# Operand moves two per tile and later loads in the attention stage of a three-stage kernel

## The chip, the cores and the metric

One core of a Trainium2 chip runs the kernel. The metric is the device time of one execution in microseconds (us), the median of several runs. The profile is one further execution, recorded by the hardware profiler, with the time of every instruction from the start of the span.

## The reference, cut to what matters

```python
# attention: B=2, H=8, S=768, D=64
q_bits = (einsum('bhsd,dk->bhsk', q, proj) > 0); k_bits likewise     # 6 bits
mask = q_bucket[..., :, None] == k_bucket[..., None, :]
scores = where(mask, matmul(q, k^T) / sqrt(D), -1e9)
x = softmax(scores) @ v            # -> [1536, 512]
# first expert layer: all 8 experts, weighted by a Sinkhorn-balanced P
x = sum_e P[:, e] * (relu(x @ w1[e]) @ w2[e])
# second expert layer: each token goes to one expert, 192 tokens each
out[mask_e] = relu(x[mask_e] @ w1b[e]) @ w2b[e]
```

The change touches the attention alone. Heads with other buckets are not cut away: the bucket test is added to the scores as 64 further rows of the product.

## The kernel before

The attention works on *pairs* of heads. There are 8 pairs (n = 0 to 7), each with 12 *tiles* (r = 0 to 11): 2 heads by 6 blocks of 128 queries. Tile t of the whole run is 12n + r; the main loop (L408 on) has 96 of them and some more to drain the pipeline. In each tile the table PLANS says in which order the steps are written, and with which lag; the engines follow that order by hand, each in its own queue, with waits only where data or a buffer demand it. The steps that matter here:

- `qk` (L283): TensorE (PE) makes the scores S from two operand pairs, S<-ka,qa and S<-kb,qb. The operands of a pair of heads are four tiles qa, ka, qb, kb of 128 rows, kept twice (`ST`), so that the next pair's are built while this pair's are read.
- `soft`, `expo`, `inv`, `norm`: VectorE (DVE) takes the maximum, ScalarE (ACT) the exponential, DVE the reciprocal w (L302), GpSimd (POOL) multiplies e by w (L307).
- `tr` (L315): PE transposes e; ACT and DVE split it into ah and al; `av` (L337): PE makes O.
- `xa` with a lag of 8 tiles: ACT copies O to SBUF and SyncE (SP) issues the *exchange* DMAs that put the two heads' halves together. For the second head of a pair the copy goes to one of three tiles in turn, x1, idle and pz (L357), and two DMAs of 64 KB follow, xm<- (L358) and xc<- (L359). These fall in r = 2, 4 and 6 of the next pair. For the first head it is one DMA xc<-xm (L353), in r = 8, 10 and 0.
- `xp` with a lag of 10: POOL adds xm and xc (L369) and splits the sum (L370, L371), in r = 4, 6 and 8, ahead of work that stands later in POOL's queue, `norm` above all.
- `pp`, `pa`, `pd`: the next pair is prepared in r = 0 to 9. r = 0 and 1 transpose and split the next q into qhi and qlo, r = 2 and 3 the next k into khi and klo; r = 4 and 5 take the bits, r = 6 to 9 make the rows of the bucket test, `hot`. `stack` puts 6 *moves* of 64 x 768 floats (192 KB, SBUF to SBUF) into the list MOVES for q in r = 1, and 6 for k in r = 3. After a tile's steps `move` issues (L165) all moves that were in the list before the tile began. The hot rows go by DMAs of their own (L241): qb<-hot twice in r = 7, kb<-hot twice in r = 9.
- `pv`: the loads of q, k and v of the next pair but one, `load(n + 2, ...)`, two DMAs of 192 KB each (L82), in r = 6, 7 and 10. Pairs 6 and 7 have no such loads. In r = 6, `pv` stands ahead of `xa` in the plan.

All these DMAs are issued by SP from one queue in program order. SP waits for nothing but what an instruction needs, so it is not bound to the tiles; a DMA whose data is late keeps all behind it back.

Of the kernel before, what the change touches and what calls it, by code (L numbers as in the profile page):

```python
# [38 lines left out]
def rd(x):  # L39
    return x.bitcast(F32)  # L40
# [3 lines left out]
def kernel(ctx, tc, q, k, v, proj, wg1, w1, w2, wg2, w1b, w2b, out):  # L44
# [29 lines left out]
    def load(n, what="qkv"):  # L74
        b, hp = divmod(n, HP)
        for nm, src in (("q", q), ("k", k), ("v", v)):
            if nm in what:
                t = ap.tile([128, R, 2, D], F32, name="r" + nm, bufs=2)
                rows = (slice(0, R // 2), slice(R // 2, R)) if n == 0 and nm != "v" else (slice(0, R),)
                for rs in rows:  # L80
                    for s in range(2):
                        nc.sync.dma_start(t[:, rs, s, :], src[b, 2 * hp + s].rearrange("(p r) d -> p r d", r=R)[:, rs])  # L82
                RAW["r" + nm, n] = t
# [78 lines left out]
    def move(n=None):  # L162

        for dst, src in MOVES[:n]:
            nc.sync.dma_start(rd(dst), rd(src))  # L165
        del MOVES[:n]
# [86 lines left out]
    def prep_v(n, i):  # L253
        x = RAW["rv", n]
        if i == 0:
            VS[n] = ap.tile([128, R, 2, 2, D], F32R, name="vv", bufs=2)
        vv = VS[n]
        s = i // 2
        if i % 2 == 0:
            nc.gpsimd.tensor_tensor(vv[:, :, s, 0, :], x[:, :, s, :],  # L260
                                    zero[:, :, None].to_broadcast([128, R, D]), op=OP.add)
        else:
            nc.gpsimd.tensor_tensor(vv[:, :, s, 1, :], x[:, :, s, :], rd(vv[:, :, s, 0, :]), op=OP.subtract)
# [114 lines left out]
    def ahead_v(t):  # L378
        n, r = divmod(t, TU)
        for i in range(4):  # L380
            if t == PREP_V[i]:
                prep_v(0, i)
        if r in (8, 10) and n + 1 < NP:
            prep_v(n + 1, r // 2 - 4)
        if r in (0, 2) and 0 < n < NP:
            prep_v(n, r // 2 + 2)
        for what, at in (("q", 6), ("k", 7), ("v", 10)):
            if r == at and n + 2 < NP:
                load(n + 2, what)

    STEPS = dict(qk=qk, soft=soft, expo=expo, inv=inv, norm=norm, tr=tr, th=trh, tl=trl, av=av, xa=xa, xp=xp, pp=lambda t: ahead(t, 0), pa=lambda t: ahead(t, 1), pd=lambda t: ahead(t, 2),
                 pv=ahead_v)
    patterns()
    for i in (0, 1, 2, 3, 4, 5, 6, 8, 7, 9):
# [15 lines left out]
    for t in range(NT + max(x[1] for x in PLANS[0])):  # L410
        if t == TU:
            nc.vector.tensor_copy(wgs[:, :, :E], wgr)
            nc.vector.tensor_tensor(wgs[:, :, E:], wgr, rd(wgs[:, :, :E]), op=OP.subtract)
        due = len(MOVES)
        for nm, lag, *part in PLANS[t % 2]:
            if 0 <= t - lag < NT:
                STEPS[nm](t - lag, *part)
        if due:
            move(due)
    order.close()  # L420
    actx.close()

# [802 lines left out]
```

## Time and profile before

| what | value |
|---|---|
| median of 3 runs | 1595.63 us (1595.05 to 1595.82) |
| profiled execution: its own time | 1594.99 us |
| profiled execution: span from first to last instruction | 1591.6 us |
| PE busy | 1553.0 us (98%) |
| DVE, ACT, POOL busy | 809.0, 453.3, 272.7 us |
| attention stage in the span | about 0 to 280 us |

An engine's share is an average over all stages. A stall is read from the engine's timeline: a row there has the start and length of the instruction and, in brackets, how long the engine stood idle before it and which instruction or DMA ended that wait. "SPq" rows are DMA issues: their length is the time to issue, not the time to land.

### The profile page before, as it was taken

Reading aid. Unit: us, or ns where it says so; the run is one execution under the profiler, and the core shown is the slowest. Engines: PE = TensorE matmul, PEld = TensorE weight load, DVE = VectorE, ACT = ScalarE, POOL = GpSimd, SP = SyncE. Lnnn points to the kernel's source line nnn. Section 1 sums busy time; section 2 is a strip of 40 time slices with the busy share of each in tenths; the row PEclk is TensorE's granted clock in tenths of the full one; section 3 lists DMA queues with packets and bytes.
Section 4 is the critical chain, followed back from the end, with each engine's and each line's share of the span. In section 5 each row is a group of like instructions: output and inputs, shape, how many; then the busy total and the mean of one; then the engine's idle time right before and its main releaser. Section 6 shows DMA issues by size and latency. Waiting matters only on the chain.

```text
span 1591.6 us, 21436 instructions
## 1 busy us (share of the span) xinstructions
PE 1553.0 (98%) x8482; PEld 1318.1 (83%) x8482; DVE 809.0 (51%) x1833; ACT 453.3 (28%) x857; POOL 272.7 (17%) x316
## 2 busy tenths in 40 slices
PE   8889999999999999999999999999999999999998
PEld 7889887788888888888888888888887777888998
DVE  7878887721523324333342332134677377667533
ACT  7778886311210211221121021022121210011343
POOL 5778888020000000000000000000000000111221
PEclk9999999999999999999999999999999999999999
DMA  9657761220200110120020021011000115555531
GB/s 194 139 128 166 160 137 35 99 93 0 81 26 14 54 53 1 53 67 1 27 87 7 14 71 36 0 54 53 1 14 14 40 41 210 191 183 187 192 136 30
DMA packets 88871, 122.84 MB, mean 77 GB/s; under 512 B 44227, under 2 KB 51907, under 8 KB 88771
## 3 DMA queue, kind: packets, MB, share of 16 engines
q1 hardware_dynamic: 81280, 108.89, 23.8%
q0 software_dynamic: 2176, 6.29, 1.3%
q10 hardware_dynamic: 5314, 6.30, 1.1%
q8 instruction: 66, 1.08, 0.3%
q14 instruction: 35, 0.28, 0.1%
HBM read 83.91 MB, written 9.44 MB: 59 GB/s over the span
## 4 chain that ended last, share of the span: by engine, by line
PE 88%; DVE 3%; DMA 2%; ACT 2%; POOL 2%; issue 1%; SPq 1%; POOLq 0%; ACTq 0%; DVEq 0%
PE hp L575 32%; PE yp L594 29%; PE hp L952 5%; PE yp L896 4%; PE yp L1005 3%; PE tp L315 2%; PE O L337 2%; PE S L283 2%; PE yp L1008 1%; PE sp L1089 1%; POOL e L307 1%; PE tp L205 1%; ACT e L295 1%; PE tp L176 1%; PE yp L1010 1%
## 5 line engine op out<-in xcount | busy, mean ns | idle before, releaser
L575 PE MATMUL hp<-X,big 128*128 128x512 f32 x2304 | 530.5, 390 | 0.6 <-DVE big L445 0.6
L575 PEld LDWEIGHTS hp<-X,big 128*128 128x128 f32 x2304 | 432.9, 188 | 91.2 <-DVE big L445 1.0
L594 PE MATMUL yp<-big 128*128 128x512 f32 x2016 | 461.2, 389 | 0.0
L594 PEld LDWEIGHTS yp<-big 128*128 128x128 f32 x2016 | 378.2, 188 | 78.5
L576 ACT ACTIVATE big<-hp 128x512 fp32r<-128x512 f32 x176 | 105.2, 598 | 753.7 <-PE hp L575 753.7
L577 DVE SCALAR_TENSOR_TENSOR big<-hp,big 128x512 fp32r<-128x512 f32 x176 | 121.4, 690 | 250.3 <-ACT big L576 250.3
L599 DVE SCALAR_TENSOR_TENSOR acc<-yp,P,acc 128x512 f32<-128x512 f32 x72 | 54.1, 751 | 258.4 <-PE yp L594 258.4
L877 POOL DMA_INDIRECT raw<-x2h,who x4 | 4.2, 1038 | 949.4 <-DVE wg2b L1074 939.0
L307 POOL TENSOR_TENSOR e<-e,w 128x768 f32<-128x768 f32 x96 | 139.0, 1468 | 31.2 <-DVE w L302 24.6
L327 DVE TENSOR_TENSOR al<-tp,ah 128x512 fp32r<-128x512 f32 x144 | 98.4, 684 | 31.3 <-ACT ah L323 27.9
L315 PE MATMUL tp<-ident,e 128*128 128x128 f32 x576 | 87.5, 280 | 15.4 <-POOL e L307 15.3
L323 ACT ACTIVATE ah<-tp 128x512 fp32r<-128x512 f32 x144 | 86.4, 601 | 42.9 <-PE tp L315 40.4
L952 PE MATMUL hp<-raw,big 128*128 128x192 f32 x488 | 93.7, 338 | 1.2 <-ACT raw L930 1.2
L290 DVE TENSOR_REDUCE w<-S 128x1 f32<-128x768 f32 x96 | 91.3, 951 | 6.9 <-PE S L283 5.8
L295 ACT ACTIVATE e<-S,w 128x768 f32<-128x768 f32 x96 | 87.0, 907 | 2.1 <-DVE w L290 1.8
L315 PEld LDWEIGHTS tp<-ident,e 128*128 128x128 f32 x576 | 69.3, 145 | 17.9 <-POOL e L307 17.0
L952 PEld LDWEIGHTS hp<-raw,big 128*128 128x128 f32 x488 | 79.7, 193 | 2.7 <-ACT raw L930 1.6
L445 DVE TENSOR_TENSOR big<-raw,big 128x1024 fp32r<-128x1024 f32 x63 | 76.7, 1221 | 9.5 <-ACT big L444 9.5
L337 PE MATMUL O<-ah,vv 128*128 128x256 f32 x288 | 74.9, 289 | 1.3 <-ACT xm L352 0.9
L337 PE MATMUL O<-al,vv 128*128 128x256 f32 x288 | 74.7, 288 | 0.0
L444 ACT ACTIVATE big<-raw 128x1024 fp32r<-128x1024 f32 x63 | 64.8, 1053 | 31.4 <-DMA raw<-in_moe_w_dram 30.0
L550 DVE SCALAR_TENSOR_TENSOR junk<-acc,wg2b 128x512 bf16<-128x512 f32 x96 | 66.0, 688 | 1.9
(261 smaller groups left out, 1587.3 us busy)
## 6 DMA issues: line engine op xcount, KB each, us to landing
raw<-in_moe_w_dram SPq DMA_DIRECT2D x67, 512.0 KB, 3.5
big<-in_moe_w_dram SPq DMA_DIRECT2D x32, 1024.0 KB, 7.5
qa<-qhi SPq DMA_DIRECT2D x30, 192.0 KB, 3.8
ka<-klo SPq DMA_DIRECT2D x16, 192.0 KB, 3.4
rv<-in_v_dram SPq DMA_DIRECT2D x16, 192.0 KB, 4.4
x2h<-acc ACTq DMA_DIRECT2D x24, 128.0 KB, 1.9
x<-acc ACTq DMA_DIRECT2D x12, 256.0 KB, 3.2
qb<-qlo SPq DMA_DIRECT2D x15, 192.0 KB, 3.6
```

The costliest lines, as they stand in the source:

```text
L290: nc.vector.tensor_reduce(EN[t][:, 0, i:i + 1], Sp[i], op=OP.max, axis=AX.X, negate=True)
L295: nc.scalar.activation(e, Sp[i], AF.Exp, bias=w[:, 0, i:i + 1], scale=1.0, accum_out=w[:, 1, i:i + 1])
L307: nc.gpsimd.tensor_tensor(e, e, w[:, 3, i:i + 1].to_broadcast([128, S]), op=OP.mult)
L315: nc.tensor.transpose(p[:, y * 128:y * 128 + 128], EN[t + i][:, kt * 128:kt * 128 + 128], ident)
L323: nc.scalar.activation(ah, TP[t, x], AF.Copy)
L327: nc.vector.tensor_tensor(al, TP[t, x], rd(ah), op=OP.subtract)
L337: nc.tensor.matmul(o, VS[n][:, kt, s].rearrange("p a d -> p (a d)"), a[:, :, kt], start=(kt == 0 and a is ah), stop=(kt == R - 1 and a is al))
L575: nc.tensor.matmul(t, a, b, start=(i == 0), stop=(i == len(prods) - 1))
L576: nc.scalar.activation(hh[:, f], t, AF.Relu)
L577: nc.vector.scalar_tensor_tensor(hl[:, f], t, 0.0, rd(hh[:, f]), op0=OP.max, op1=OP.subtract)
L594: nc.tensor.matmul(t, a, b, start=(i == 0), stop=(i == len(prods) - 1))
L952: nc.tensor.matmul(opened[f], w[:, d, f * 128:f * 128 + 128], xt[:, d], start=(d == 0), stop=(d == HP - 1))
```

## The change

Two edits. The loads of the pair n + 2 move from r = 6, 7 and 10 to r = 8, 10 and 11 (the 9th, 11th and 12th tile of a pair). And after each tile at most two of the waiting moves are issued instead of all.

```diff
-        for what, at in (("q", 6), ("k", 7), ("v", 10)):
+        for what, at in (("q", 8), ("k", 10), ("v", 11)):
             if r == at and n + 2 < NP:
                 load(n + 2, what)
@@
-        if due:
-            move(due)
+        move(min(due, 2))
```

PE, DVE, ACT and POOL keep their order. SP's changes in pairs 0 to 6. In SP's queue in pair 1, from the idle exchange to the pz exchange (ka, kb, qa, qb are operand tiles of the next pair, rq the load of q), before:

```order
L358 DMA xm<-idle 64x256
L359 DMA xc<-idle 64x256
L165 DMA ka_119<-khi 64x768
L165 DMA ka_119<-klo 64x768
L165 DMA kb_121<-khi 64x768
L165 DMA ka_119<-khi 64x768
L165 DMA ka_119<-klo 64x768
L165 DMA kb_121<-khi 64x768
L82 DMA rq<-in_q_dram 128x6x64 x2
L358 DMA xm<-pz 64x256
L359 DMA xc<-pz 64x256
```

The same stretch in the change:

```order
L358 DMA xm<-idle 64x256
L359 DMA xc<-idle 64x256
L165 DMA qa_118<-qhi 64x768
L165 DMA qb_120<-qlo 64x768
L165 DMA ka_119<-khi 64x768
L165 DMA ka_119<-klo 64x768
L358 DMA xm<-pz 64x256
L359 DMA xc<-pz 64x256
```

Between the two exchanges stand four moves, where six moves and the two q loads stood; ahead of the idle exchange stand four moves, where there were six.

In SP's queue in pair 1, behind the pz exchange up to the hot rows of kb (rk is the load of k), before:

```order
L82 DMA rk<-in_k_dram 128x6x64 x2
L241 DMA qb_120<-hot_831 64x768 x2
L353 DMA xc<-xm 64x256
L241 DMA kb_121<-hot_906 64x768 x2
L82 DMA rv<-in_v_dram 128x6x64 x2
```

And in the change:

```order
L165 DMA kb_121<-khi 64x768
L165 DMA ka_119<-khi 64x768
L241 DMA qb_120<-hot_824 64x768 x2
L165 DMA ka_119<-klo 64x768
L165 DMA kb_121<-khi 64x768
L82 DMA rq<-in_q_dram 128x6x64 x2
L353 DMA xc<-xm 64x256
L241 DMA kb_121<-hot_903 64x768 x2
L82 DMA rk<-in_k_dram 128x6x64 x2
```

Four k moves and the q loads now stand between the pz exchange and kb<-hot; the k loads went behind it, and the v loads behind those.

## Rows read from the trace of the kernel before

**Rows 1.** The page, part 1: busy time, share, instructions of each engine.
```profile
PE 1553.0 (98%) x8482; PEld 1318.1 (83%) x8482; DVE 809.0 (51%) x1833; ACT 453.3 (28%) x857; POOL 272.7 (17%) x316
```

**Rows 2.** Waits of PE, 10 to 280 us: total us, times, longest.
```profile
PE tp L315 <- POOL e L307: 15.3, 7, 4.1
...
PE S L283 <- DMA kb<-hot: 2.3, 1, 2.3
```

**Rows 3.** Timeline of PE: start, us, instruction, [idle before, releaser].
```profile
42.31 0.58 PE L283 MATMUL S<-kb,qb 128*128 128x512 f32 x2 [2.33 <-DMA kb<-hot]
...
71.23 0.66 PE L315 MATMUL tp<-ident,e 128*128 128x128 f32 x4 [2.81 <-POOL e L307]
106.03 1.02 PE L315 MATMUL tp<-ident,e 128*128 128x128 f32 x4 [4.05 <-POOL e L307]
...
138.47 0.66 PE L315 MATMUL tp<-ident,e 128*128 128x128 f32 x4 [1.70 <-POOL e L307]
...
170.59 0.74 PE L315 MATMUL tp<-ident,e 128*128 128x128 f32 x4 [2.70 <-POOL e L307]
203.90 0.66 PE L315 MATMUL tp<-ident,e 128*128 128x128 f32 x4 [2.57 <-POOL e L307]
...
237.59 0.51 PE L283 MATMUL S<-kb,qb 128*128 128x512 f32 x2
```

**Rows 4.** Waits of POOL, 10 to 280 us; then two rows of its timeline.
```profile
POOL e L307 <- DVE w L302: 24.6, 17, 8.6
...
POOL xm L369 <- DMA xc<-pz: 6.7, 2, 3.8
POOL xm L369 <- DMA xm<-pz: 6.6, 3, 2.6
...
134.75 0.73 POOL L369 TENSOR_TENSOR xm<-xm,xc 128x256 f32<-128x256 f32 x1 [1.44 <-DMA xm<-pz]
...
230.73 0.74 POOL L369 TENSOR_TENSOR xm<-xm,xc 128x256 f32<-128x256 f32 x1
```

**Rows 5.** Chain of waits, 126 to 140 us: start, us, link.
```profile
130.95 3.43 DMA xm<-pz
```

**Rows 6.** Timeline of ACT in pair 3.
```profile
127.83 0.38 ACT L357 ACTIVATE pz<-O 128x256 f32<-128x256 f32 x1 [0.82 <-PE O L337]
```

**Rows 7.** Timeline of SP, DMA issues in pairs 1, 3, 4 and 6.
```profile
48.91 0.46 SPq L358 DMA_DIRECT2D xm<-x  x1
...
117.27 0.46 SPq L358 DMA_DIRECT2D xm<-x  x1
...
124.47 0.59 SPq L165 DMA_DIRECT2D ka<-khi  x1
...
128.76 2.08 SPq L82 DMA_DIRECT2D rq<-in_q_dram  x2
130.95 0.58 SPq L358 DMA_DIRECT2D xm<-pz  x1
...
148.47 0.46 SPq L358 DMA_DIRECT2D xm<-x  x1
...
215.16 0.46 SPq L358 DMA_DIRECT2D xm<-x  x1
```

**Rows 8.** Windows: stretch, busy by engine, then granted PE clock, DMA share, GB/s.
```profile
71.20:77.20 6.00, 5.97 (x34) 5.75 (x35) 2.90 (x4) 3.46 (x8) 6.00 (x5) 0.72 0.42 72
...
138.40:144.40 6.00, 5.93 (x46) 5.68 (x47) 4.52 (x8) 4.77 (x11) 6.00 (x6) 1.00 0.59 102
...
164.00:170.00 6.00, 3.89 (x30) 3.50 (x28) 4.85 (x10) 4.61 (x11) 3.36 (x5) 1.00 0.98 221
...
226.00:238.00 12.00, 12.00 (x93) 11.45 (x92) 10.87 (x21) 11.57 (x26) 11.38 (x11) 1.00 0.62 152
```

**Rows 9.** Line 241 (hot rows): its 28 landings; then SP's issue in pair 6.
```profile
DMA to landing us min/median/max: 2.7/4.2/5.9
...
229.29 1.10 SPq L241 DMA_DIRECT2D qb<-hot  x2
```

## The prediction

> **What bounds the kernel now.** I read the page first: TensorE (PE) is busy 1553.0 of the 1591.6 us span [rows 1], so an edit of DMA order can only pay where PE stands still. The list of PE's waits over the attention part (10 to 280 us, where the edited code runs) comes next. It has two entries above noise that touch the edit: 15.3 us in 7 waits for POOL's normalisation of e (L307), and one of 2.3 us for the rows kb<-hot [rows 2]. The timeline of PE then gives place and size of each [rows 3]: one stall in each of pairs 1 to 5, of 2.81, 4.05, 1.70, 2.70 and 2.57 us, in sum 13.83 us, and the 2.33 us at the start of pair 1. The other two waits of the seven, 1.5 us together, lie after 250 us in pair 7, where the edit moves nothing.
>
> Why is POOL late there? POOL's waits name the exchange DMAs of the tile pz: 6.7 + 6.6 us in 5 waits [rows 4]. In pair 3, POOL stood 1.44 us until 134.75 for xm<-pz, then had the three exchange operations to do and after them the normalisation for which PE stood 1.70 us. The chain of waits has the same DMA as a link of 3.43 us from 130.95 [rows 5]. And why was the DMA issued at 130.95? ScalarE had written pz at 128.21 (127.83 + 0.38) [rows 6]. The SyncE timeline [rows 7] shows the queue issuing without a break: the six k moves from 124.47 to 128.76 (4.29 us, 0.72 us each), two rq loads of 2.08 us, and only then pz. So the exchange is 2.7 us late in its issue, behind six moves and two loads that nobody needs yet.
>
> Pair 6 is the control that the kernel itself contains: no pair 8 exists, so its loads are absent, while its twelve moves stand as before. There POOL starts the pz sum at 230.73 with no wait [rows 4], and PE is busy 12.00 of 12.00 us from 226 to 238 [rows 8]. Taking the loads alone from in front of the exchange was enough.
>
> **The change part by part.** No instruction is added or removed on any engine: the same DMAs (12 moves, 6 loads, 4 hot rows, 9 exchanges a pair) are issued in another order, so the busy terms are zero and all of it is waits. SP does not know tiles; it issues as soon as its waits allow, and "two per tile" only means that four moves stand between two exchanges.
>
> *Exchange pz.* By the order listing it now has four moves between itself and the idle exchange, in place of six moves and two loads. Even if they began no earlier than the k moves did, SP would be through them at 124.47 + 4 x 0.72 = 127.35, before pz is written at 128.21. So pz leaves at about 128.25, 2.7 us earlier. With the old 3.43 us to landing [rows 5] it lands at 131.7, its sister xc<-pz 0.6 us later at 132.3; POOL was ready at 134.75 - 1.44 = 133.31. The wait is covered with 1.0 us to spare in pair 3; in the pairs with longer waits the exchange stood behind the same fourteen DMAs (twelve moves and two loads), so I expect the same there, and the control agrees. Gain: the five stalls, 13.83 us. What is next in line for PE is its own work, as pair 6 shows.
>
> *The clock.* In the 6 us after the stalls of pairs 1, 2, 4 and 5 the granted clock is 0.72, with 34 or 35 matmuls done; after the 1.70 us of pair 3 it is 1.00, with 46 matmuls [rows 8]; of the four, the first stands there. So four stalls were followed by a stretch in part on the 1.2 GHz level, and the one in pair 3 by 2.4 GHz throughout. The price comes from the periods between one pair's exchange xm<-x and the next [rows 7]: pair 3 takes 148.47 - 117.27 = 31.20 us, less its stall 29.50. Pairs 1 to 5 take 215.16 - 48.91 = 166.25 us; less stalls 152.42; less 5 x 29.50 = 147.50 leaves 4.92 us, 1.23 us for each of the four. I take it as gained too.
>
> *Hot rows of kb.* This is the new danger. Before, kb<-hot had the loads of k and the hot rows of qb close ahead. Now the q loads and the last k moves stand there, and the k loads go behind. I lay the new order onto pair 6, which runs free. SP issues qb<-hot at 229.29, when the values are there [rows 9]. In an almost empty queue a 192 KB move lands 2.7 us after issue, the lowest of 28 [rows 9]: 232.0. Behind it in the stream are the second qb<-hot, two moves, two q loads, one 64 KB exchange, and then kb<-hot. The engines move 221 GB/s when they are full (share 0.98) [rows 8], that is 0.89 us for 192 KB and 0.30 for 64 KB. So kb<-hot lands at 232.0 + 6 x 0.89 + 0.30 = 237.6. PE wants it at 237.59 [rows 3]: a tie. From the other side: SP needs four issues of 0.6, the q loads' 2.08 and 0.6 for the exchange, so it issues kb<-hot at 229.29 + 5.1 = 234.4; with the shortest, median and longest landing of the 28 (2.7, 4.2, 5.9 us) it is there at 237.1, 238.6 or 240.3, so PE waits 0, 1.0 or 2.7 us. Between the tie of the stream sum and the 1.0 us of the median I take 0.5 us, in each of pairs 1 to 5: 2.5 us lost.
>
> The Trainium skill, "DMA: Bandwidth & Descriptors", section "Anatomy of one DMA", prices a DMA at a fixed 2.0 us plus its bytes at 436 GB/s (a fit for DMAs issued from GpSimd), whatever stands ahead of it; by that kb<-hot would be there 2.45 us after issue, at 236.9, as an estimate, and no new wait would arise. The median of 4.2 us against the lowest of 2.7 speaks for a queue instead, so I keep the queue.
>
> *Start of pair 1.* kb<-hot for pair 1 is issued in pair 0 and made PE wait 2.33 us [rows 3]. It now has two loads fewer ahead, 2 x 0.89 = 1.8 us earlier at the landing. I leave 0.5 us of the stall: 1.8 us gained. *Later users of the loads.* q, k and v come 2, 3 and 1 tiles later; a tile is 29.50 / 12 = 2.46 us, and they are read 4, 4 and 9 tiles after issue (9.8 us or more), against landings of a few us. Nothing, unless SP itself falls behind by more than two tiles.
>
> **Sum.** 13.83 + 4.92 + 1.8 - 2.5 = 18.1 us. The profiled run took 1594.99 us (span 1591.6, the rest outside it), 0.6 below the median 1595.63. From its own time: 1576.9; at the median: 1577.5. I give 1577.5.
>
> **Rivals.** (a) *No new wait at all*: kb<-hot always in time. Then 13.83 + 4.92 + 2.33 = 21.1 us, 1574.5. For it: the 0.0 us of the tie. Against it: the median landing. The price of the Trainium skill, quoted above, would give this case. (b) *The wait moves over to kb<-hot*: 1.5 to 2.5 us at six places, short of a fallen clock. 21.1 - 6 x 2.0 = 9.1 us, 1586.5. For it: the longest landing of 5.9 us, seen where the queue was full, and kb<-hot has already stopped PE once. Against it: the queue is nearly empty when qb<-hot leaves. (c) *Slower*: the same wait beyond 2.8 us, place the first tile of each pair, with the clock falling each time as after stalls of 2.57 and more. Each then costs wait + 1.23 us; at 3.5 us it is 6 x 4.73 = 28.4 against 21.1 gained, 7.3 us slower, 1602.9. The point from which it decides is 6 x (w + 1.23) = 21.1, w = 2.3; over 0.2% slower from w = 2.8, which needs a landing of 6.1 us, above all 28. (d) *The edit does not free POOL*: POOL also waits 24.6 us for DVE's w [rows 4], and if that were next in line the stalls would stay: 1595. Against it: pair 6 has the same DVE work and no stall.
>
> **How the numbers follow.** A difference of 0.2% (3.2 us) is about what can be told from no change. Forecast (16 to 20 us gained) 0.53, (a) 0.17, (b) 0.20, (c) 0.05, (d) and waits near 2.5 us, ending within 0.2%, 0.05. Faster therefore 0.90, same 0.05, slower 0.05. The range: from (a) with 1 us for what the sum has not seen, 1573.5, up to kb<-hot 2.0 us late everywhere, (b), with 1 us on it, 1587.5; what lies outside is (c), (d), the upper part of (b) and the lower part of (a), together about 2 in 10.
>
> **What would show it.** Right: in the waits of PE no POOL e L307 entry above 1 us before 250 us; xm<-pz issued within 0.1 us of ScalarE's write; POOL without waits for pz; clock 1.00 from 60 to 250 us; the period from pair to pair near 30.0 us. A PE wait for kb<-hot (or for qb) of 0 to 1 us at the first tile of pairs 1 to 6 is my 2.5 us term; if it reads 2 us or more, that term is wrong and (b) or (c) holds. If POOL waits for DVE where it waited for pz and PE still stands, (d) holds. If the periods without stalls stay at 30.7 us with the clock at 1.00, the clock term is wrong.

## The result and the profile after

The changed kernel takes 1579.08 us (median of 5 runs, 1577.10 to 1584.43) against 1595.35 us of the kernel before beside it (5 runs). The ratio is 0.9908 with a 95% interval of 0.9883 to 0.9932: faster, by 0.7 to 1.2%. The forecast was 1577.5 us with a range of 1573.5 to 1587.5. The profiled execution took 1579.08 us, its span 1577.2 us, 14.4 us less than the 1591.6 us before.

Where did it go? A mark that every version has is PE's first product after the attention, sp<-X,wgs (L488 before, L487 after, since the edit removes a line). Timelines of PE, first of the kernel before, then of the changed one:

```profile
274.35 0.39 PE L488 MATMUL sp<-X,wgs 128*16 128x512 f32 x1
```

```profile
259.49 0.39 PE L487 MATMUL sp<-X,wgs 128*16 128x512 f32 x1
```

All of it is in the attention: 14.86 us there, and 0.5 us given back in the 1317 us behind it. (This is one execution of each kernel. A later one of the changed kernel, e6 below, has the mark at 256.38.) PE's waits, 10 to 275 us, answer to [rows 2] (total us, times, longest):

```profile
PE S L283 <- DMA kb<-hot: 5.6, 4, 2.5
...
PE S L283 <- issue: 2.3, 2, 1.6
PE tp L315 <- POOL e L307: 1.4, 2, 0.7
```

Of the 15.3 us for e, 1.4 us are left, both waits after 240 us in pair 7. In their place stands what was 2.3 us before: the product S<-kb,qb. The timeline of PE, which answers to [rows 3], has all six waits, one at the first tile of each of pairs 1 to 6:

```profile
41.40 0.59 PE L283 MATMUL S<-kb,qb 128*128 128x512 f32 x2 [1.59 <-issue]
...
71.26 0.59 PE L283 MATMUL S<-kb,qb 128*128 128x512 f32 x2 [0.67 <-issue]
102.09 0.61 PE L283 MATMUL S<-kb,qb 128*128 128x512 f32 x2 [1.63 <-DMA kb<-hot]
...
133.78 0.59 PE L283 MATMUL S<-kb,qb 128*128 128x512 f32 x2 [2.48 <-DMA kb<-hot]
...
163.68 0.58 PE L283 MATMUL S<-kb,qb 128*128 128x512 f32 x2 [0.72 <-DMA kb<-hot]
193.66 0.59 PE L283 MATMUL S<-kb,qb 128*128 128x512 f32 x2 [0.79 <-DMA kb<-hot]
```

Two of them carry the name "issue" where the profile found no releaser. It is the same product at the same place, and PE went on 0.13 and 0.07 us after the first kb<-hot had landed (36.37 + 4.9 = 41.27 and 67.49 + 3.7 = 71.19). So I count all six as waits for the hot rows of kb: 7.88 us, 6.29 of them at the ends of pairs 1 to 5. (Below, too, this wait is counted by its instruction; the releaser that the profile names is sometimes the DMA that landed next to it.)

ACT and then SP in pair 3, which answer to [rows 6, 7], show the exchange leaving at once. pz is written at 119.29 + 0.39 = 119.68, and the DMA goes at 119.73. It had gone 2.7 us late before.

```profile
119.29 0.39 ACT L357 ACTIVATE pz<-O 128x256 f32<-128x256 f32 x1 [0.82 <-PE O L337]
```

```profile
119.73 0.46 SPq L358 DMA_DIRECT2D xm<-pz  x1
...
122.84 1.10 SPq L241 DMA_DIRECT2D qb<-hot  x2
123.98 0.59 SPq L165 DMA_DIRECT2D ka<-klo  x1
...
125.26 1.91 SPq L82 DMA_DIRECT2D rq<-in_q_dram  x2
127.28 0.60 SPq L353 DMA_DIRECT2D xc<-xm  x1
127.98 1.18 SPq L241 DMA_DIRECT2D kb<-hot  x2
```

POOL's waits, as in [rows 4], have no line for pz any more; the windows, as in [rows 8], have the clock at 1.00 behind the waits of pairs 1 to 3 (the stretch, busy times by engine, then clock, DMA share, GB/s):

```profile
71.20:77.20 6.00, 5.94 (x46) 5.75 (x47) 5.11 (x10) 5.00 (x13) 5.31 (x5) 1.00 0.88 142
102.10:108.10 6.00, 6.00 (x47) 5.79 (x48) 5.16 (x10) 4.27 (x10) 4.33 (x5) 1.00 0.48 96
133.80:139.80 6.00, 6.00 (x47) 5.79 (x48) 5.20 (x10) 4.31 (x10) 3.50 (x4) 1.00 0.36 79
```

### The profile page after: what moved, and what is told of

The parts are those of the page before. It is cut to its first block, busy times and chain, and to the rows that moved or that the text cites. A ratio compares the mean times of both kernels' runs of the same rounds, so it can differ in the third digit from the quotient of the medians.

```text
span 1577.2 us, 21432 instructions
## 1 busy us (share of the span) xinstructions
PE 1546.5 (98%) x8482; PEld 1312.5 (83%) x8482; DVE 805.7 (51%) x1833; ACT 453.5 (29%) x857; POOL 272.0 (17%) x316
## 3 DMA queue, kind: packets, MB, share of 16 engines
q0 software_dynamic: 2176, 6.29, 1.3%
## 4 chain that ended last, share of the span: by engine, by line
PE 90%; ACT 3%; DMA 2%; DVE 2%; issue 1%; POOL 1%; SPq 0%; ACTq 0%; POOLq 0%; DVEq 0%
PE hp L574 33%; PE yp L593 29%; PE hp L951 5%; PE yp L895 4%; PE S L283 3%; PE yp L1004 3%; PE O L337 3%; PE tp L315 2%; PE yp L1007 1%; PE sp L1088 1%; ACT e L295 1%; PE tp L205 1%; DMA kb<-hot 1%; PE yp L1009 1%; PE tp L176 1%
## 5 line engine op out<-in xcount | busy, mean ns | idle before, releaser
L327 DVE TENSOR_TENSOR al<-tp,ah 128x512 fp32r<-128x512 f32 x144 | 98.4, 684 | 14.4 <-ACT ah L323 10.9
L443 ACT ACTIVATE big<-raw 128x1024 fp32r<-128x1024 f32 x63 | 64.9, 1054 | 30.8 <-DMA raw<-in_moe_w_dram 29.5
```

The lines of the kernel that those rows point to most:

```text
L327: nc.vector.tensor_tensor(al, TP[t, x], rd(ah), op=OP.subtract)
```

## The experiments

The theory: SP's one queue and the DMA engines behind it work off transfers in order, so a row that PE or POOL needs pays for every transfer that was put in shortly ahead of it, in a later issue or in a longer landing. By it the gain comes from clearing the way of pz, and what is left comes from what now stands ahead of kb<-hot. Rivals: that the bursts of moves did the harm and not the loads; that one of the two edits does nothing; that kb<-hot costs the same wherever it stands.

The end of the attention (the mark above) and the wait for kb are from each kernel's profile.

| kernel | median us | ratio to before, 95% | attention ends | wait at S<-kb,qb, pairs 1 to 6 |
|---|---|---|---|---|
| before | 1595.35 | | 274.35 | 2.3 (start of pair 1) |
| the change | 1579.08 | 0.9908 (0.9883 to 0.9932) | 259.49 | 7.9 |
| e1, loads alone | 1573.52 | 0.9872 (0.9851 to 0.9894) | 255.53 | none |
| e2, moves alone | 1582.01 | 0.9930 (0.9910 to 0.9950) | 262.80 | 8.7 |
| e3, no load ahead of kb<-hot | 1577.03 | 0.9887 (0.9868 to 0.9905) | 255.10 | none |
| e4, four loads ahead | 1598.85 | 1.0030 (1.0014 to 1.0046) | 278.83 | 19.2 |
| e5, q load alone | 1586.61 | 0.9954 (0.9938 to 0.9970) | 266.96 | 10.2 |
| e6, the change again | 1576.16 | 0.9893 (0.9875 to 0.9912) | 256.38 | 5.5 |
| e7, loads alone again | 1573.56 | 0.9867 (0.9845 to 0.9888) | 255.49 | none |

Each ratio is to runs of the kernel before on the same chip: median 1593.18 us for e1 to e4, 1593.26 us for e5 to e7. So the times of different groups are not to be set beside each other; the gain over the own median before is 16.3 us for the change, 19.7 for e1, 17.1 for e6 and 19.7 for e7.

**e1, the loads alone.** The moves go six at once, as before:

```diff
-        move(min(due, 2))
+        move(due)
```

> The later loads alone; the moves go six at once as before. Theory (queue): what stands ahead in SP's one queue sets the landing, 0.9 us for each 192 KB. The pz exchange has six moves but no loads ahead, as in pair 6 of the kernel before, so POOL does not wait for pz and PE has no stall for e; and behind qb<-hot there are two moves fewer, so kb<-hot lands 1.8 us earlier than in the change: PE waits for it under 0.5 us in pairs 1 to 6 together with the start of pair 1 under 1 us, against 7.9 us in the change. Time 1571 to 1575 us. Rival (bursts): the six moves in one piece are what makes the exchange late. Then the stalls of 1.7 to 4 us for e stay and the time is 1588 to 1595. Rival (fixed): kb<-hot costs the same wherever it stands; then 1579 with the same 7.9 us.

Measured: 1573.52 us, in the theory's range. PE's waits from 38 to 250 us have no line for kb<-hot; the largest is again e, with 2.6 us in four waits, none over 0.8 us (1.2 us of it in pairs 1 and 5, the rest in pair 7). POOL still waits for pz in two places, where the theory had none:

```profile
PE tp L315 <- POOL e L307: 2.6, 4, 0.8
POOL xm L369 <- DMA xc<-pz: 1.2, 2, 0.8
```

So the bursts do little harm here: behind six moves in one piece pz leaves 0.9 us after ACT has written it in pair 3 (117.72 + 0.38 = 118.10, issued at 119.02), and that is nearly always early enough. And kb<-hot is on time. SP's timeline in pair 3 has three rows between the pz exchange and kb<-hot, where the change has four moves more:

```profile
119.02 0.88 SPq L358 DMA_DIRECT2D xm<-pz  x1
119.94 0.95 SPq L359 DMA_DIRECT2D xc<-pz  x1
121.27 1.10 SPq L241 DMA_DIRECT2D qb<-hot  x2
122.42 1.34 SPq L82 DMA_DIRECT2D rq<-in_q_dram  x2
123.87 0.58 SPq L353 DMA_DIRECT2D xc<-xm  x1
125.76 1.15 SPq L241 DMA_DIRECT2D kb<-hot  x2
```

kb<-hot is issued 4.49 us after qb<-hot here, against 5.14 us in the change. Here SP stands ready and issues as soon as ACT has written the rows (125.16 + 0.57 = 125.73); in the change they are written at 127.29 and SP is still at work on the queue until 127.88. ACT in e1, then in the change:

```profile
125.16 0.57 ACT L236 ACTIVATE hot<-tp,cb 128x384 fp32r<-128x384 f32 x1
```

```profile
126.72 0.57 ACT L236 ACTIVATE hot<-tp,cb 128x384 fp32r<-128x384 f32 x1
```

From issue to landing the hot rows take 2.7 / 3.1 / 4.4 us in e1 (lowest, median, longest; the trace holds the landing of 16 of the 28), 2.7 / 3.6 / 5.2 us in the change (of 17):

```profile
DMA to landing us min/median/max: 2.7/3.1/4.4
```

```profile
DMA to landing us min/median/max: 2.7/3.6/5.2
```

**e2, the moves alone.** The loads stay where they were:

```diff
-        for what, at in (("q", 8), ("k", 10), ("v", 11)):
+        for what, at in (("q", 6), ("k", 7), ("v", 10)):
```

> The moves two per tile alone; the loads stay in r = 6, 7 and 10. Theory (queue): the pz exchange has four moves and two loads between itself and the idle exchange; SP is through them before ScalarE has written pz, and the pz rows land about 1.7 us before POOL wants them, so the stalls for e go here too. Ahead of kb<-hot stand the same number of transfers as in the change (the k loads in place of the q loads), so PE waits for kb<-hot by 4 to 8 us in sum. Time 1576 to 1581. Rival (loads): only taking the loads away frees the exchange; then the five stalls stay, at 1 to 3 us each, and the time is 1585 to 1593.

Measured: 1582.01 us, 1 us over the theory's range, and the mechanism as it says. The waits for e fall to 1.1 us between 38 and 250 us, though both q loads stand directly ahead of pz. So either edit alone clears the way of pz, which the rival (loads) denied. The wait for kb is 8.7 us, as large as in the change:

```profile
PE S L283 <- issue: 3.7, 3, 2.4
PE S L283 <- DMA rv<-in_v_dram: 3.4, 1, 3.4
PE S L283 <- DMA kb<-hot: 1.6, 2, 0.9
PE tp L315 <- POOL e L307: 1.1, 2, 0.7
```

The three lines for S are all S<-kb,qb; the 3.4 us are the start of pair 1, with both loads ahead and two moves behind qb<-hot.

**e3, no load between qb<-hot and kb<-hot.** The change with

```diff
-        for what, at in (("q", 8), ("k", 10), ("v", 11)):
+        for what, at in (("q", 10), ("k", 11), ("v", 11)):
```

> The change with the loads of q, k and v in r = 10, 11 and 11, so that no load stands between qb<-hot and kb<-hot. Theory (queue): kb<-hot lands 1.8 us earlier, PE's wait for it falls from 7.9 us in sum to under 1.5 us; the q loads land at about the time PE transposes them (0 to 1 us of a new wait for rq in each of pairs 2 to 6). Time 1572 to 1578. Rival (fixed): the wait for kb<-hot stays at 6 us or more, 1579.

Measured: 1577.03 us, in the theory's range. The wait for kb is gone, against the rival (fixed), and the expected new one is there: PE's transposes of q wait 3.4 us in six places, 1.4 us in the longest, where up to 1 us was expected.

```profile
PE tp L176 <- DMA rq<-in_q_dram: 3.4, 6, 1.4
```

**e4, the suspected cost doubled.** The k loads also ahead of kb<-hot:

```diff
-        for what, at in (("q", 8), ("k", 10), ("v", 11)):
+        for what, at in (("q", 8), ("k", 8), ("v", 11)):
```

> The change with the k loads also in r = 8, so that four loads instead of two stand ahead of kb<-hot: the suspected cost doubled. Theory (queue): kb<-hot lands 1.8 us later, so PE's wait for it at the start of each of pairs 1 to 6 grows from 0.7 to 2.5 us to 2.5 to 4.3 us, 18 us in sum against 7.9, and the granted clock falls behind the longer ones (1.2 us more each). Time 1589 to 1597. Rival (fixed): the place does not matter, 1577 to 1581.

Measured: 1598.85 us, slower than before by 0.14 to 0.46%. The wait is 19.2 us in six places (18 us expected):

```profile
PE S L283 <- DMA kb<-hot: 11.1, 4, 3.0
PE S L283 <- DMA xc<-xm: 8.1, 2, 4.2
```

Two more transfers of 192 KB ahead cost 11.3 us of wait over six pairs, 0.94 us each. The place where they cost it was not expected: it is SP's issue, not the landing. kb<-hot leaves 6.7 to 8.6 us after qb<-hot in pairs 0 to 5, against 5.1 to 5.4 in the change, while the landings that the trace holds for it there (3.9 to 4.5 us) are no longer than in the change (3.7 to 5.2). In pair 3 the one exchange behind the loads took SP 2.62 us to issue, where it took 0.60 in the change:

```profile
131.31 1.10 SPq L241 DMA_DIRECT2D qb<-hot  x2
...
135.68 1.40 SPq L82 DMA_DIRECT2D rk<-in_k_dram  x2
137.19 2.62 SPq L353 DMA_DIRECT2D xc<-xm  x1
139.91 1.18 SPq L241 DMA_DIRECT2D kb<-hot  x2
```

The attention ends 19.3 us later than in the change; the 8 us beyond the waits go with the clock, which reads 0.72 and 0.50 behind the longest two (3.83 and 4.22 us):

```profile
109.00:115.00 6.00, 6.00 (x36) 5.82 (x37) 3.82 (x7) 2.80 (x6) 3.11 (x3) 0.72 0.23 49
144.00:150.00 6.00, 6.00 (x25) 5.71 (x26) 3.88 (x7) 2.34 (x5) 2.92 (x3) 0.50 0.24 54
```

This is the prediction's rival (c), reached by one load: the mean wait is 3.2 us, and (c) was to be over 0.2% slower from 2.8 us. By (c)'s sum, 6 x (3.2 + 1.23) - 21.1, it would be 5.5 us slower; its median is 5.7 us above that of the kernel before beside it.

**e5, the q load alone.** The kernel before with one number changed:

```diff
-        for what, at in (("q", 6), ("k", 7), ("v", 10)):
+        for what, at in (("q", 8), ("k", 7), ("v", 10)):
```

> The kernel before with one load moved: q from r = 6 to r = 8; k and v stay in r = 7 and 10, the moves go six at once. Theory (queue): the two q loads were the last straw ahead of pz, so the stalls for e go as in e1 (POOL waits for pz under 1 us in each pair); and since the last k moves are not behind qb<-hot, kb<-hot has the q loads and one exchange behind qb<-hot, as in e1, with the k loads ahead of qb<-hot, where the queue has room. PE waits for kb<-hot under 1 us in pairs 2 to 6. Time 1572 to 1577. Rival: the k loads, 2 x 0.9 us more ahead of kb<-hot than in e1, come through in full: 1 to 1.5 us of wait in each pair, 1579 to 1583.

Measured: 1586.61 us. My expectation fell; the rival's mechanism held, at more than its price. pz is free (POOL waits 0.2 us for it), but PE waits 10.2 us for kb:

```profile
PE S L283 <- DMA kb<-hot: 10.2, 6, 3.5
```

I had counted the transfers behind qb<-hot alone. Here the k loads stand ahead of it, and they count too: kb<-hot takes 4.3 to 7.0 us from issue to landing in pairs 0 to 5, against 2.8 to 4.0 us in e1 (of those that the traces hold). That the queue does not run dry between pz and the hot rows, so that everything since then adds up, is how I read it; no run here measures the queue itself.

**e6 and e7, the change and e1 again, on one chip.**

> The change again, beside e7 on the same chip: 1577 to 1581, kb<-hot waits of 5 to 9 us in sum. Were the e1 gain a matter of the chip or the hour, e6 and e7 would be equal.

> The later loads alone again, beside e6: 1571 to 1576, that is 4 to 8 us under e6, with no waits for kb<-hot above 0.5 us.

e6 came to 1576.16 us, 0.8 us under its range, with 5.5 us of wait for kb; e7 to 1573.56 us with none, 2.6 us under e6 where 4 to 8 were expected. Against its own runs of the kernel before the loads alone gain 3.4 us (e1, the change) and 2.6 us (e7, e6) more, but the intervals of the ratios overlap, so that e1 is faster than the change is not shown. That the loads alone have no wait for kb and the change 5.5 to 7.9 us is shown twice. Not all of it reaches the time: without these waits the attention ends 4.0 us earlier in e1 than in the change, and only 0.9 us earlier in e7 than in e6. e1 beats the kernel before clearly and, with the lowest time in either group, is the version to keep.

## Why the prediction was right, point by point

**The bound and the place.** Right. The five stalls for e were 13.83 us and are gone; e1, e2 and e5 each remove them by clearing the way of pz in a different manner, and pair 6 of the kernel before had foretold that taking the loads away is enough.

**pz leaves 2.7 us earlier.** Right: 0.05 us after ACT's write, with no POOL wait for pz in the profile after.

**The clock, 4.92 us.** Right: the clock reads 1.00 over each of pairs 1 to 5, and more than the term was gained. The periods of the exchange xm<-x from pair 1 to pair 6, as in [rows 7], now are:

```profile
48.01 0.51 SPq L358 DMA_DIRECT2D xm<-x  x1
...
200.26 0.51 SPq L358 DMA_DIRECT2D xm<-x  x1
```

That is 152.25 us for five pairs, less 6.29 us of waits 145.96, or 29.19 us a pair. I had taken 29.50 us from the one period of the kernel before whose clock read 1.00 behind its stall. So 166.25 - 13.83 - 145.96 = 6.46 us went besides the stalls, 1.5 us more than the term. This 1.5 us is not the clock: in pair 3 it read 1.00 before and after, and PE's busy time went from 29.50 to 29.18 us all the same. It goes with the moves: at a clock of 1.00, PE is busy 29.0 to 29.2 us a pair where they go two per tile (19 of the 20 pairs 1 to 5 of the change, e2, e3 and e6; 29.4 in the other), and 29.4 to 29.5 us where they go six at once (all ten of e1 and e7). What in PE's work is shorter is not shown. Pair 3 before, in the change and in e1:

```profile
117.27:148.47 31.20, 29.50 (x224) 27.93 (x222) 27.76 (x49) 25.93 (x57) 26.73 (x25) 1.00 0.71 159
```

```profile
108.71:140.37 31.66, 29.18 (x223) 27.85 (x222) 26.56 (x50) 25.87 (x56) 26.91 (x25) 1.00 0.70 157
```

```profile
107.26:136.75 29.49, 29.45 (x223) 27.81 (x222) 27.43 (x50) 25.85 (x57) 26.90 (x26) 1.00 0.72 168
```

**kb<-hot, 2.5 us for pairs 1 to 5 and 0.5 us at the start of pair 1.** The mechanism was right, the size was not: 6.29 and 1.59 us. Three of the six waits are over the 1 us that was named for this term, and one, 2.48 us, is past the 2 us at which the prediction itself called the term wrong. The step that failed is the choice between the tie of the stream sum and the 1.0 us of the median landing: the five waits at the ends of pairs 1 to 5 have a mean of 1.26 us. SP issued kb<-hot 5.14 us after qb<-hot in pair 3, as worked out (5.1). But the landing took 3.7 us in pair 1, 3.8 us in pair 4 and 4.9 us for pair 1's start, where the tie would have needed 3.2 us. For pairs 2 and 3 the chain of waits has it, from issue to landing:

```profile
97.38 4.66 DMA kb<-hot
```

```profile
127.98 5.66 DMA kb<-hot
```

The stream sum started from an empty queue and a full rate of 221 GB/s, and e5 speaks against the first of these: with two more transfers ahead of qb<-hot the wait for kb grew. The landings that the sum drew on were also fewer than it says: the trace before holds a landing for 13 of the 28 issues of [rows 9], so the longest of them, 5.9 us, bounds nothing: e5 has one of 7.0 us. The whole stretch from 60 to 72 us moved 199 GB/s in the profile after:

```profile
60.00:72.00 12.00, 11.33 (x87) 10.63 (x86) 10.12 (x18) 11.66 (x26) 11.84 (x11) 1.00 0.95 199
```

Why it is 0.7 us in three pairs, 1.6 and 2.5 us in two and 1.6 us at the start stays open; e6 has the same places at other lengths (1.47 us at 100 us, 1.35 at 131, 1.04 at 191).

**The fixed price of a DMA.** The landings of the hot rows in the change run from 2.7 to 5.7 us, PE waits 7.9 us in all for those of kb, and e4 adds 0.94 us for each transfer put ahead. The Trainium skill ("DMA: Bandwidth & Descriptors", "Anatomy of one DMA") gives a DMA 2.0 us plus its bytes at 436 GB/s, a fit for DMAs issued from GpSimd without a term for what stands ahead; by it, as an estimate, each would land after 2.45 us and no wait for kb would arise. For these DMAs, issued by SP, the trace does not agree; it comes near only at the lowest landing, 2.7 us.

**The sum.** Forecast 18.1 us; the profiled times differ by 15.9 us and the spans by 14.4. By parts in the attention: 13.83 + 6.46 - 6.29 + 0.74 (start of pair 1, 2.33 - 1.59) = 14.74 of the measured 14.86 us. The kb term took 4.9 us more than allotted, and the 1.5 us of shorter PE work, which no term had, gave part of it back; that the whole came this near is to that extent luck.

**The rivals.** (a), no new wait, is not what the change does, but it is what e1 does, with a gain of 19.7 us over its own median before where 21.1 was worked out. (b), 2.0 us at six places, is what the change is two thirds of the way to (1.3 us each), and e5 nearly is (1.7); there the gain is only 6.7 us, not 9.1 or more, because in e5 the clock did fall behind two of the waits. (c) came true in e4, but not by the landing of 6.1 us that it named (its own terms, 3.2 + 2.8, make 6.0): there the issue came later. (d), POOL held by DVE anyway, did not happen anywhere.

## What to carry to other kernels

In a queue that one engine issues, list for each consumer that waits what was issued in the time just ahead of the row it needs, and move away from there what has a late deadline; the deadline, not the even spread, is what the order should follow. The six moves in one burst cost little (1.2 us of stalls for e in pairs 1 to 6 of e1), because most of the time after the idle exchange was free for them; spread out, four of them came to lie between pz and the hot rows of kb, and a new wait came with them. When a profile has one unit that lacks the suspected cause (here the pair without loads), read it first: it is an experiment already made.

## What the runs showed of the hardware that I had not expected

The clock does not follow the length of the one gap before it. In e2 the 3.42 us wait at 43.5 us was followed by 0.72, but in e4 one of 2.94 us at 42.8 us by 1.00, while before the change one of 2.81 us was followed by 0.72 [rows 3, 8]. In e5 two waits of the same 2.13 us, at 137.8 and 169.4 us, were followed by 1.00 and 0.72. The windows of e4, e2 and e5:

```profile
42.70:48.70 6.00, 5.91 (x46) 5.72 (x47) 5.09 (x10) 4.21 (x10) 3.22 (x3) 1.00 0.25 50
```

```profile
43.50:49.50 6.00, 5.96 (x35) 5.76 (x36) 3.91 (x7) 2.76 (x6) 3.27 (x3) 0.72 0.07 18
```

```profile
137.80:143.80 6.00, 6.00 (x47) 5.78 (x48) 5.14 (x10) 4.26 (x10) 3.83 (x4) 1.00 0.19 38
...
169.30:175.30 6.00, 5.93 (x35) 5.69 (x36) 3.91 (x7) 2.71 (x6) 3.85 (x4) 0.72 0.23 45
```

Behind the attention, where all kernels run the same instructions, the rest of the span still differs: 1315.0 us in e2 and 1315.3 in e1, 1317.2 before, 1318.6 in e7, 1320.2 in e3 (span less the end of the attention). It goes with the clock from 1360 to 1420 us: 0.97 in e1 and e2, 0.94 before, 0.90 in e7, 0.89 in e3 (windows of 60 us at one distance behind the end of the attention read the same within 0.01). No run here steered that clock, so why it differs is open; it is as large as the difference between e1 and the change, and reason enough to compare such versions by the end of the stage that was edited.
